# A linear-attention block beside a GEGLU feed-forward: the attention output in four and a half array passes instead of five

## The chip, the cores and the metric

The kernel runs on one core of one Trainium2 chip. The metric is the device time of one execution in microseconds (us); the median of nine runs of the kernel before is 516.6 us, with the lowest at 516.16 and the highest at 517.53. The profile is that of one execution, which took 516.65 us. Its recorded span, from the first to the last instruction that the profile shows, is 514.6 us, so about 2.0 us lie around it.

## The reference

With S = 2048 tokens, D = 576 features, H = 32 heads of Dh = 18 and F = 4608:

```python
xn = layernorm(x)
q, k, v = split_heads(xn @ wqkv)            # (H, S, Dh)
phi = lambda t: where(t > 0, t + 1, exp(t)) + 1e-6
kv  = einsum("hsd,hse->hde", phi(k), v)     # one 18 x 18 matrix for each head
z   = phi(k).sum over s                     # (H, Dh)
num = einsum("hqd,hde->hqe", phi(q), kv)
den = einsum("hqd,hd->hq", phi(q), z) + 1e-6
A   = merge_heads(num / den) @ wo
B   = (gelu(xn @ w_gate) * (xn @ w_up)) @ w_down
out = x + A + B
```

Since the attention is linear, the kernel folds kv and wo into one 576 x 576 matrix M (for each head, kv of the head times the head's 18 rows of wo). With phi(q) divided by its denominators beforehand, the attention output is A = (phi(q)/den) @ M: one more contraction over 576 rows, whose result is added to that of the feed-forward in the same accumulator.

## The kernel before, in words

**Stages.** The first part, up to 68.4 us of the span, does the layer norm, the projections of q and k, the Gram products that give k^T v, and the small matrices kvT (18 x 18 blocks, masked) and zb (z on all partitions). The feed-forward then goes through the tokens in four chunks (`sc`) of 512. In each chunk there are two stages.

- **Gate and up** (`gu_pair`, line 548). 18 blocks `k`, each of two units of 128 hidden columns. A unit makes a gate and an up product in two PSUM banks. The contraction over 576 rows is done by `_Unit` in 64-row tiles of the array: one matmul on rows 0 to 63 (`LO`) and one on rows 64 to 127 (`HI`) run side by side, on different banks (line 309). ScalarE then computes the gelu (line 575), and VectorE multiplies and writes `hT` (line 576).
- **Down** (`down_tile`, line 591). Four tiles `j` of 128 tokens, each in two halves of 288 output columns. A half is 36 full-array passes over `hT` and `w_down` (line 604), then five passes with `pqT` (phi(q)/den, transposed) against `m_sb` (M) (line 609), all into one bank; then VectorE adds x (line 612) and SP sends the tile out (lines 614 and 616).

**The five passes.** The 32 heads are packed 7, 7, 7, 7 and 4 to a chunk (`HCH`), so chunks 0 to 3 fill 126 of the 128 rows, and chunk 4 fills 72. Each chunk is one pass.

**M.** `m_stage` (line 581) makes M, chunk by chunk, within the first half of the first down tile of the first token chunk: before the passes f = 0, 6, 12, 18 and 24 it issues two matmuls of kvT against wo (line 586) into banks that the accumulator does not use, and ScalarE copies each to `m_sb` (line 589).

**Denominators.** For each token tile `n` there are four jobs, kept in the list `den_jobs` (line 546): `den_mul` (line 367), `den_inv` (line 373), `den_scale` (line 379), which are VectorE work and write the padded tile `pn`, and `den_transpose` (line 395), a transposing DMA from `pn` to `pqT` on SP's queue. `gu_pair` takes one job after each unit of the blocks 1 to 16 (line 577). That is 32 jobs in a chunk, so all 64 are done within the first two chunks. The three `pn` buffers are filled with zeros once (line 532), since columns 126 and 127 of the first four chunks, and 72 to 127 of the last, are never written.

**Queues and order.** Nothing is scheduled by a planner in this part: every engine runs its instructions in the order of the code. All loads of weights, the transposes and the stores go through SP's queue. A block's weights are loaded three blocks ahead (`load_gu(blk + NWBUF - 1, i)`, line 565), wo in block 1 of the first chunk (line 569), and w_down in slices in blocks 2 to 13 (line 571). PSUM banks are handed out in a fixed ring of eight (`banks`, line 296), two to each unit and one to each half of a down tile. When a unit's first half is done, `p1` leaves a marker on POOL's queue (line 318), and `p2` waits for it before its row tiles change banks.

Of the kernel before, what the change touches and what calls it, by code (L numbers as in the profile page):

```python
# [9 lines left out]
ALU = mybir.AluOpType  # L10
BF16 = mybir.dt.bfloat16
# [4 lines left out]
P = 128  # L16
HP = 64
S = 2048
D = 576
H = 32  # L20
DH = 18
F = 4608
NS = S // P
NF = F // P
SC = 512
NSC = S // SC
TPC = SC // P
HALF = D // 2
KT = 5
HCH = [7, 7, 7, 7, 4]  # L30
HOFF = [0, 7, 14, 21, 28]
NCH = len(HCH)
CR = 7 * DH
EPS_LN = 1e-5
EPS_ATT = 1e-6
GUB = 2
# [21 lines left out]
def kernel(  # L58
# [11 lines left out]
    nc = tc.nc  # L70
# [5 lines left out]
    out_view = out.flatten_outer_dims().rearrange("(p n) d -> p n d", n=NS)  # L76
# [5 lines left out]
    fwork = ctx.enter_context(tc.tile_pool(name="fwork", bufs=3))  # L82
    psum = ctx.enter_context(tc.tile_pool(name="psum", bufs=1, space=PSUM))

    ps_all = psum.tile([P, 8, 512], F32, name="ps_all")
# [4 lines left out]
    x_sb = persist.tile([P, NS, D], BF16, name="x_sb")  # L90
# [46 lines left out]
    pqT = persist.tile([P, NCH, S], BF16, name="pqT")  # L137
# [5 lines left out]
    hT = h_store[:].rearrange("p (f t) -> p f t", f=NF)  # L143
# [8 lines left out]
    def load_gu(i, part):  # L152

        if i >= NSC * NF // GUB:
            return
        f0 = GUB * (i % (NF // GUB))
        c0, c1 = f0 * P, (f0 + GUB) * P
        if part == 0:
            gu_blocks[i] = (wg_bufs.next(), wu_bufs.next(), wr_bufs.next())
        wg, wu, wr = gu_blocks[i]  # L160
        if part == 0:
            nc.sync.dma_start(wg[:], B_w_gate[0:512, c0:c1].rearrange("(kt p) c -> p kt c", p=P))
            nc.sync.dma_start(wr[0:HP, :], B_w_gate[512:576, c0:c1])
        else:
            nc.sync.dma_start(wu[:], B_w_up[0:512, c0:c1].rearrange("(kt p) c -> p kt c", p=P))
            nc.sync.dma_start(wr[HP:P, :], B_w_up[512:576, c0:c1])
# [13 lines left out]
        out=bm3, in_=bm3, compare_op=ALU.is_ge, fill=0.0,  # L180
# [3 lines left out]
        out=bm3, in_=bm3, compare_op=ALU.is_ge, fill=0.0,  # L184
# [109 lines left out]
    LO, HI = slice(0, HP), slice(HP, P)  # L294
    SYNC = mybir.DependencyInfo(mybir.DependencyClass.Sync, mybir.DependencyReason.DATA)
    banks = _Ring([4, 5, 6, 7, 2, 3, 0, 1])

    class _Unit:
# [5 lines left out]
        def __init__(self, outs, lhs, rhs, relay, first=(4, 0, 1, 2, 3), then=(0, 1, 2, 3)):  # L304
            self.outs, self.lhs, self.rhs, self.relay = outs, lhs, rhs, relay
            self.first, self.then = first, then
# [55 lines left out]
    def heads(ap):  # L362
        return ap.rearrange("p (h e) -> p h e", e=DH)
# [14 lines left out]

    def den_scale(n):
        pn = den_pn[n] = pn_bufs.next()  # L380
        for c0, c1 in ((0, 4), (4, 5)):
            h0, h1 = HOFF[c0], HOFF[c1 - 1] + HCH[c1 - 1]
            nh = HCH[c0]

            def chunked(ap):
                return ap.rearrange("p (c h) e -> p c h e", h=nh)

            nc.vector.scalar_tensor_tensor(  # L388
                out=pn[:].rearrange("p (c t) -> p c t", t=P)[:, c0:c1, :nh * DH].rearrange("p c (h e) -> p c h e", e=DH),
                in0=chunked(heads(pq[:, n, h0 * DH:h1 * DH])), scalar=EPS_ATT,  # L390
                in1=chunked(den_d[n][:, h0:h1].unsqueeze(2).to_broadcast([P, h1 - h0, DH])),
                op0=ALU.add, op1=ALU.mult,
            )

    def den_transpose(n):
        nc.sync.dma_start_transpose(pqT[:, :, n * P:(n + 1) * P], den_pn[n][:])
# [20 lines left out]
    for n in range(NS):  # L417
# [7 lines left out]
        if n < TD:  # L425
            for i, (k0, k1, eng) in enumerate([(0, 3, "ACT"), (3, KT, "ACT" if n else "DVE")]):
                b = TP_BANK[n] - i
# [97 lines left out]
    wd_pool = ctx.enter_context(tc.tile_pool(name="wd", bufs=1))  # L525
    wd_sb = wd_pool.tile([P, NF, D], BF16, name="wd_sb")
    wo2 = wd_pool.tile([P, NCH, D], BF16, name="wo2")
    m_sb = wd_pool.tile([P, NCH, D], BF16, name="m_sb")
    dwork = ctx.enter_context(tc.tile_pool(name="dwork", bufs=1))
    pn_bufs = _Ring([dwork.tile([P, NCH * P], BF16, name=f"pn{i}") for i in range(3)])  # L530
    for pn in pn_bufs.tiles:
        nc.gpsimd.memset(pn[:], 0.0)

    def load_wo():
        nc.sync.dma_start(wo2[:CR, 0:4, :], A_wo[0:4 * CR, :].rearrange("(c p) j -> p c j", p=CR))
        nc.sync.dma_start(wo2[:D - 4 * CR, 4, :], A_wo[4 * CR:D, :])
    wd_loaded = [0]

    def load_wd_slice():
        f0 = wd_loaded[0]  # L540
        if f0 < NF:
            nc.sync.dma_start(wd_sb[:, f0:f0 + WDS, :], wd_view[:, f0:f0 + WDS, :])
            wd_loaded[0] += WDS


    den_jobs = [(job, n) for n in range(NS) for job in (den_mul, den_inv, den_scale, den_transpose)]

    def gu_pair(sc, k):
        cs = slice(sc * SC, (sc + 1) * SC)
        blk = sc * (NF // GUB) + k  # L550
        wg, wu, wr = gu_blocks.pop(blk)
        units = []
        for i in range(GUB):
            b = [banks.next(), banks.next()]
            fcol = slice(i * P, (i + 1) * P)

            def lhs(a, rows, kt, fcol=fcol):
                if kt == 4:
                    return wr[rows, fcol]
                return (wg, wu)[a][rows, kt, fcol]  # L560

            u = _Unit([ps_all[:, b[0], :], ps_all[:, b[1], :]], lhs, lambda a, rows, kt: xnT[rows, kt, cs],
                      nc.sync if blk == 0 else nc.gpsimd)
            if blk > 0:
                load_gu(blk + NWBUF - 1, i)
            u.p1()
            units.append((b, u))
        if sc == 0 and k == 1:
            load_wo()
        elif sc == 0 and k >= 2:  # L570
            load_wd_slice()
        for i, (b, u) in enumerate(units):
            u.p2()
            gl = fwork.tile([P, SC], F32, name="gl")
            nc.scalar.activation(out=gl[:], in_=ps_all[:, b[0], :], func=ACT.Gelu_apprx_tanh)  # L575
            nc.vector.tensor_tensor(out=hT[:, GUB * k + i, :], in0=ps_all[:, b[1], :], in1=gl[:], op=ALU.mult)  # L576
            if den_jobs and 0 < k < NF // GUB - 1:
                job, n = den_jobs.pop(0)
                job(n)

    def m_stage(c, acc_bank):
        rows = DH * HCH[c]
        for hf in range(2):
            b = (acc_bank + 2 + (2 * c + hf) % 6) % 8
            hs = slice(hf * HALF, (hf + 1) * HALF)
            nc.tensor.matmul(  # L586
                ps_all[:rows, b, :HALF], lhsT=kvT[:rows, c, :rows], rhs=wo2[:rows, c, hs], start=True, stop=True,
            )
            nc.scalar.copy(out=m_sb[:rows, c, hs], in_=ps_all[:rows, b, :HALF])

    def down_tile(sc, j, hooks):
        n = sc * TPC + j
        ts_ = slice(n * P, (n + 1) * P)
        res = fwork.tile([P, D], BF16, name="res")
        last = n == NS - 1
        for hf in range(2):
            hs = slice(hf * HALF, (hf + 1) * HALF)
            todo = hooks.pop(0) if hooks else {}
            acc_bank = banks.next()
            acc = ps_all[:, acc_bank, :HALF]  # L600
            for f in range(NF):
                if f in todo:
                    todo[f](acc_bank)
                nc.tensor.matmul(  # L604
                    acc, lhsT=hT[:, f, j * P:(j + 1) * P], rhs=wd_sb[:, f, hs], start=(f == 0), stop=False,
                )
            for c in range(NCH):
                rows = DH * HCH[c]
                nc.tensor.matmul(  # L609
                    acc, lhsT=pqT[:rows, c, ts_], rhs=m_sb[:rows, c, hs], start=False, stop=(c == NCH - 1),  # L610
                )
            nc.vector.tensor_tensor(out=res[:, hs], in0=acc, in1=x_sb[:, n, hs], op=ALU.add)  # L612
            if last:
                nc.sync.dma_start(out_view[:, n, hs], res[:, hs])
        if not last:
            nc.sync.dma_start(out_view[:, n, :], res[:])

    for sc in range(NSC):
        for k in range(NF // GUB):
            gu_pair(sc, k)  # L620
        while wd_loaded[0] < NF:
            load_wd_slice()

        hooks = [{6 * c_: (lambda b, c_=c_: m_stage(c_, b)) for c_ in range(NCH)} if sc == 0 else {}]
        for j in range(TPC):
            down_tile(sc, j, hooks)


# [28 lines left out]
```

## Time and profile before

| what | value |
|---|---|
| median of nine runs | 516.6 us |
| the profiled execution | 516.65 us, span 514.6 us |
| TensorE busy, granted clock | 509.2 us (99%), 1.00 |
| VectorE, ScalarE, POOL busy | 203.0, 136.9, 8.4 us |
| gate and up, each of the four chunks | 70.0 to 70.1 us |
| down, first chunk | 42.0 us |
| down, each of the other chunks | 40.3 to 40.4 us |
| passes of line 604, line 609, line 586 | 1152, 160, 10 |
| DMA share while gate and up of chunks 0, 1, 2, 3 run | 1.01, 0.61, 0.54, 0.46 |

The chain that ended last is TensorE for 97% of the span. The durations of single matmuls in the profile (286 ns for a pass with 288 columns) hold the pipeline's depth; what a pass adds is the distance from one start to the next. DMA share is the mean busy share of the 16 DMA engines.

### The profile page before, as it was taken

The numbers are of one execution on the slowest core, as the hardware profiler recorded it, in microseconds if no ns is written. First come the engines' busy times: TensorE is split into PE (matmuls) and PEld (weight loads), VectorE is DVE, ScalarE is ACT, GpSimd is POOL, SyncE is SP. The second block draws the span as 40 slices with busy tenths as digits, with TensorE's granted clock in tenths as the row PEclk, the third lists the DMA queues.
The fourth block names the chain that finished last, engine by engine and source line by source line (L and its number), as shares of the span: only waits on it lengthen the run. The fifth ranks groups of instructions, "written<-read, shape, count | busy, mean of one in ns | idle before, by whom it ended". The sixth has DMA issues, their size and how long they took to land.

```text
span 514.6 us, 10566 instructions
## 1 busy us (share of the span) xinstructions
PE 509.2 (99%) x4487; PEld 309.3 (60%) x4487; DVE 203.0 (39%) x414; ACT 136.9 (27%) x267; POOL 8.4 (2%) x26
## 2 busy tenths in 40 slices
PE   8999999999999999999999999999999999999997
PEld 7888854444587744444677644444777444445775
DVE  7886447667501046676301133333101234333100
ACT  5887522232410022232100023322000133232000
POOL 3001000000000000000000000000000000000000
PEclk9999999999999999999999999999999999999999
DMA  6543929999900055666400255555100454540000
GB/s 209 144 65 62 247 57 245 272 290 288 206 11 13 13 150 147 183 173 167 128 11 24 59 160 157 145 156 146 33 12 13 129 160 141 160 117 1 13 11 24
DMA packets 118745, 61.02 MB, mean 119 GB/s; under 512 B 25514, under 2 KB 117866, under 8 KB 118698
## 3 DMA queue, kind: packets, MB, share of 16 engines
q1 hardware_dynamic: 118554, 60.20, 44.5%
q8 instruction: 35, 0.57, 0.5%
q10 hardware_dynamic: 144, 0.15, 0.1%
q14 instruction: 12, 0.10, 0.1%
HBM read 52.79 MB, written 2.36 MB: 107 GB/s over the span
## 4 chain that ended last, share of the span: by engine, by line
PE 97%; DMA 1%; SPq 0%; DVE 0%; ACT 0%; issue 0%
PE ps_all L309 54%; PE ps_all L604 27%; PE ps_all L254 7%; PE ps_all L285 4%; PE ps_all L609 4%; DMA wqkv_sb<-in_A_wqkv_dram 1%; PE ps_all L356 0%; PE ps_all L586 0%; SPq L93 0%; DVE hT L576 0%; ACT gl L575 0%; SPq L108 0%; DVE res L612 0%; SPq L107 0%; PE ps_all L346 0%
## 5 line engine op out<-in xcount | busy, mean ns | idle before, releaser
L309 PE MATMUL ps_all<-xnT,wg 64*128 64x512 bf16 x1152 | 271.9, 376 | 0.0
L309 PE MATMUL ps_all<-xnT,wu 64*128 64x512 bf16 x1152 | 271.5, 376 | 0.0
L575 ACT ACTIVATE gl<-ps_all 128x512 f32<-128x512 f32 x144 | 86.0, 597 | 313.6 <-PE ps_all L309 308.8
L576 DVE TENSOR_TENSOR hT<-ps_all,gl 128x512 bf16<-128x512 f32 x144 | 99.3, 690 | 143.6 <-ACT gl L575 143.2
L309 PEld LDWEIGHTS <-wu 64*128 64x128 bf16 x1152 | 108.3, 94 | 68.3
L309 PEld LDWEIGHTS <-wg 64*128 64x128 bf16 x1152 | 108.3, 94 | 67.7
L604 PE MATMUL ps_all<-wd_sb,hT 128*128 128x288 bf16 x1152 | 147.0, 286 | 0.0
L604 PEld LDWEIGHTS <-hT 128*128 128x128 bf16 x1152 | 112.3, 98 | 30.0 <-issue 1.6
L612 DVE TENSOR_TENSOR res<-ps_all,x_sb 128x288 bf16<-128x288 f32 x32 | 14.6, 458 | 144.9 <-PE ps_all L609 144.9
L309 PE MATMUL ps_all<-xnT,wr 64*128 64x512 bf16 x288 | 54.6, 376 | 0.0
L254 PE MATMUL ps_all<-wqkv_sb,xnT 128*128 128x288 bf16 x320 | 42.1, 286 | 0.4 <-ACT xnT L243 0.3
L254 PEld LDWEIGHTS <-xnT 128*128 128x128 bf16 x320 | 30.6, 98 | 7.8 <-ACT xnT L243 0.5
L261 ACT ACTIVATE phi_e<-ps_all,neg 128x288 f32<-128x288 f32 x64 | 30.8, 496 | 9.0 <-PE ps_all L254 6.3
L609 PE MATMUL ps_all<-m_sb,pqT 126*128 126x288 bf16 (+1 forms) x160 | 24.9, 285 | 0.0
L309 PEld LDWEIGHTS <-wr 64*128 64x128 bf16 x288 | 14.0, 94 | 17.4 <-issue 0.7
L285 PE MATMUL ps_all<-hT,xn 128*128 128x288 bf16 (+4 forms) x176 | 22.6, 275 | 0.0
L285 PEld LDWEIGHTS <-xn 128*128 128x128 bf16 (+1 forms) x176 | 17.6, 101 | 3.9
L609 PEld LDWEIGHTS <-pqT 126*128 126x128 bf16 (+1 forms) x160 | 15.5, 97 | 4.1
L266 DVE SCALAR_TENSOR_TENSOR pq<-phi_e,ps_all 128x288 bf16<-128x288 f32 x32 | 14.2, 448 | 7.7 <-ACT phi_e L261 7.2
L266 DVE SCALAR_TENSOR_TENSOR hT<-phi_e,ps_all 128x288 bf16<-128x288 f32 x32 | 14.1, 450 | 2.4 <-ACT phi_e L261 2.3
L203 DVE BATCH_NORM_STATS2 stats<-x_sb 128x6 f32<-128x288 bf16 x32 | 13.6, 440 | 1.9 <-DMA x_sb<-in_A_x_dram 1.9
L388 DVE SCALAR_TENSOR_TENSOR pn<-pq,den_d 128x504 bf16<-128x504 bf16 (+1 forms) x32 | 13.1, 449 | 0.0
(52 smaller groups left out, 96.9 us busy)
## 6 DMA issues: line engine op xcount, KB each, us to landing
wg<-in_B_w_gate_dram SPq DMA_DIRECT2D x72, 256.0 KB, 3.0
wu<-in_B_w_up_dram SPq DMA_DIRECT2D x72, 256.0 KB, 3.6
wd_sb<-in_B_w_down_dram SPq DMA_DIRECT2D x12, 432.0 KB, 4.9
wr<-in_B_w_gate_dram SPq DMA_DIRECT2D x72, 32.0 KB, 2.9
wr<-in_B_w_up_dram SPq DMA_DIRECT2D x72, 32.0 KB, 3.1
out_dram<-res SPq DMA_DIRECT2D x15, 144.0 KB, 1.8
wqkv_sb<-in_A_wqkv_dram SPq DMA_DIRECT2D x3, 576.0 KB, 5.6
x_sb<-in_A_x_dram SPq DMA_DIRECT2D x5, 288.0 KB, 3.2
```

Of the source, the lines that this page charges most:

```text
L203: nc.vector.bn_stats(out=ln_raw[n][:, h, :], in_=x_sb[:, n, h * HALF:(h + 1) * HALF])
L254: nc.tensor.matmul(ps_all[:, KQ_BANK[which] + hf, :HALF], lhsT=xnT[:, kt, n * P:(n + 1) * P], rhs=wqkv_sb[:, kt, c:c + HALF], start=(kt == ...
L261: nc.scalar.activation(out=e[:], in_=ps_all[:, KQ_BANK[which] + hf, :HALF], func=ACT.Exp, bias=neg1[:], scale=1.0,)
L266: nc.vector.scalar_tensor_tensor(out=(pq, pk)[which][:, n, hf * HALF:(hf + 1) * HALF], in0=e_tiles[n, which, hf][:], scalar=1.0, in1=ps_al ...
L285: nc.tensor.matmul(ps_all[:m, b, col:col + w], lhsT=xn[:, n, j0:j0 + m], rhs=pk[:, n, d0:d0 + w], start=(n == 0 and col == 0), stop=(n == ...
L309: return nc.tensor.matmul(self.outs[i], lhsT=self.lhs(i, rows, kt), rhs=self.rhs(i, rows, kt), start=start, stop=stop, skip_group_check=True,)
L388: nc.vector.scalar_tensor_tensor(out=pn[:].rearrange("p (c t) -> p c t", t=P)[:, c0:c1, :nh * DH].rearrange("p c (h e) -> p c h e", e=DH), ...
L575: nc.scalar.activation(out=gl[:], in_=ps_all[:, b[0], :], func=ACT.Gelu_apprx_tanh)
L576: nc.vector.tensor_tensor(out=hT[:, GUB * k + i, :], in0=ps_all[:, b[1], :], in1=gl[:], op=ALU.mult)
L604: nc.tensor.matmul(acc, lhsT=hT[:, f, j * P:(j + 1) * P], rhs=wd_sb[:, f, hs], start=(f == 0), stop=False,)
L609: nc.tensor.matmul(acc, lhsT=pqT[:rows, c, ts_], rhs=m_sb[:rows, c, hs], start=False, stop=(c == NCH - 1),)
L612: nc.vector.tensor_tensor(out=res[:, hs], in0=acc, in1=x_sb[:, n, hs], op=ALU.add)
```

## The change

- Chunk 4 of phi(q) and M keeps 64 rows; its other eight rows go to the free rows 126 and 127 of chunks 0 to 3. `den_scale` does that for phi(q) with one small copy, and with a second one repeats the 64 columns in columns 64 to 127, so that after the transpose they stand on rows 0 to 63 and on rows 64 to 127 of `pqT`. With every column written, the zero fill of `pn` goes.
- For M, chunk 4 is computed early (`m_last_product`, after block 4 of the first chunk) into a tile of its own, `m_last`. Two DMAs after block 7 bring its last eight rows to rows 126 and 127 of chunks 0 to 3 of `m_sb`, and two after block 9 bring the first 64 rows to both halves of chunk 4.
- A half of a down tile then has four full passes with `pqT` instead of five. The 64 rows of chunk 4 are done by `pair()`: one matmul on rows 0 to 63 for the left half, and one on rows 64 to 127 for the right half, on different banks, once for each tile. For tiles 0 and 1 the pairs open the accumulation, directly behind the gate-and-up stage. For tiles 2 and 3 they close it, after the last pass of tile 3 and directly ahead of the next gate-and-up stage; in the last chunk they open it, ahead of tile 2.
- All eight banks of a down stage are taken at its start. Chunks 0 to 3 of M are made ahead of passes 8, 14, 20 and 26, in the banks of tiles 2 and 3.
- `gu_pair` takes one job of `den_jobs` for each block instead of one for each unit: 16 in a chunk, so that a chunk's own four token tiles are prepared in it, and the jobs spread over all four chunks.

```diff
@@ den_scale
+        nc.vector.tensor_copy(
+            out=pn_c[:, 0:4, CR:P], in_=pn_c[:, 4, HP:HP + 8].rearrange("p (i c) -> p c i", c=4),
+        )
+        nc.vector.tensor_copy(out=pn_c[:, 4, HP:P], in_=pn_c[:, 4, 0:HP])
@@
+    m_last = wd_pool.tile([P, D], BF16, name="m_last")
...
-    for pn in pn_bufs.tiles:
-        nc.gpsimd.memset(pn[:], 0.0)
@@ gu_pair
-            if den_jobs and 0 < k < NF // GUB - 1:
+            if den_jobs and i == 1 and 0 < k < NF // GUB - 1:
                 job, n = den_jobs.pop(0)
                 job(n)
@@
-    def m_stage(c, acc_bank):
+    def m_product(c, bank):
...
+    def m_last_product():
+        two = [banks.next(), banks.next()]
+        m_product(4, lambda hf: two[hf])
+
+    def m_last_tails():
+        for i in range(2):
+            nc.sync.dma_start(m_sb[CR + i:CR + i + 1, 0:4, :], m_last[HP + 4 * i:HP + 4 * i + 4, :])
+
+    def m_last_rows():
+        for rows in (LO, HI):
+            nc.sync.dma_start(m_sb[rows, 4, :], m_last[0:HP, :])
+
+    m_last_steps = {4: m_last_product, 7: m_last_tails, 9: m_last_rows}
...
+        def pair(self):
+            for hf, rows in ((0, LO), (1, HI)):
+                nc.tensor.matmul(
+                    self.acc(hf), lhsT=pqT[rows, 4, self.ts], rhs=m_sb[rows, 4, HALVES[hf]],
+                    start=not self.opened, stop=self.opened, skip_group_check=True,
+                )
+            self.opened = True
...
-            for c in range(NCH):
-                rows = DH * HCH[c]
+            for c in range(4):
                 nc.tensor.matmul(
-                    acc, lhsT=pqT[:rows, c, ts_], rhs=m_sb[:rows, c, hs], start=False, stop=(c == NCH - 1),
+                    self.acc(hf), lhsT=pqT[:, c, self.ts], rhs=m_sb[:, c, HALVES[hf]],
+                    start=False, stop=(paired and c == 3), skip_group_check=True,
                 )
...
     for sc in range(NSC):
         for k in range(NF // GUB):
             gu_pair(sc, k)
+            if sc == 0 and k in m_last_steps:
+                m_last_steps[k]()
...
+        tiles = [_DownTile(sc * TPC + j) for j in range(TPC)]
+        tiles[0].pair()
+        tiles[1].pair()
+        spare = tiles[2].banks + tiles[3].banks
+        hooks = {8 + 6 * c: (lambda c=c: m_product(c, lambda hf: spare[(2 * c + hf) % 4])) for c in range(4)} if sc == 0 else {}
+        for j, t in enumerate(tiles):
+            if j == 2 and sc == NSC - 1:
+                tiles[2].pair()
+                tiles[3].pair()
+            closed = t.opened
+            for hf in range(2):
+                t.down(hf, hooks if j == hf == 0 else {})
+                if closed:
+                    t.add(hf)
+        for t in tiles[2:]:
+            if sc < NSC - 1:
+                t.opened = True
+                t.pair()
+                for hf in range(2):
+                    t.add(hf)
```

More of the change, by code (lines that the diff above doesn't have):

```diff
@@ L380, in den_scale @@
         pn = den_pn[n] = pn_bufs.next()
+        pn_c = pn[:].rearrange("p (c t) -> p c t", t=P)
         for c0, c1 in ((0, 4), (4, 5)):
@@ L388, in den_scale @@
             nc.vector.scalar_tensor_tensor(
-                out=pn[:].rearrange("p (c t) -> p c t", t=P)[:, c0:c1, :nh * DH].rearrange("p c (h e) -> p c h e", e=DH),
+                out=pn_c[:, c0:c1, :nh * DH].rearrange("p c (h e) -> p c h e", e=DH),
                 in0=chunked(heads(pq[:, n, h0 * DH:h1 * DH])), scalar=EPS_ATT,
@@ L576, in gu_pair @@
             nc.vector.tensor_tensor(out=hT[:, GUB * k + i, :], in0=ps_all[:, b[1], :], in1=gl[:], op=ALU.mult)
-            if den_jobs and 0 < k < NF // GUB - 1:
+            if den_jobs and i == 1 and 0 < k < NF // GUB - 1:
                 job, n = den_jobs.pop(0)
                 job(n)
-    def m_stage(c, acc_bank):
+    def m_product(c, bank):
         rows = DH * HCH[c]
         for hf in range(2):
-            b = (acc_bank + 2 + (2 * c + hf) % 6) % 8
+            b = bank(hf)
             hs = slice(hf * HALF, (hf + 1) * HALF)
@@ L588, in m_stage @@
             )
[L589 to L600, printed above, removed]
+            nc.scalar.copy(out=m_sb[:rows, c, hs] if c < 4 else m_last[:rows, hs], in_=ps_all[:rows, b, :HALF])
@@ new lines, in m_last_product @@
+    def m_last_product():
[8 more added lines that the diff above has]
+    m_last_steps = {4: m_last_product, 7: m_last_tails, 9: m_last_rows}
+    HALVES = [slice(0, HALF), slice(HALF, D)]
@@ new lines, with __init__, acc, down @@
+    class _DownTile:
+        def __init__(self, n):
+            self.n, self.ts = n, slice(n * P, (n + 1) * P)
+            self.banks = [banks.next(), banks.next()]
+            self.opened = False
+        def acc(self, hf):
+            return ps_all[:, self.banks[hf], :HALF]
+        def pair(self):
[5 more added lines that the diff above has]
+            self.opened = True
+        def down(self, hf, todo):
+            paired = self.opened
+            j = self.n % TPC
@@ L601, in down_tile @@
             for f in range(NF):
                 if f in todo:
-                    todo[f](acc_bank)
+                    todo[f]()
                 nc.tensor.matmul(
-                    acc, lhsT=hT[:, f, j * P:(j + 1) * P], rhs=wd_sb[:, f, hs], start=(f == 0), stop=False,
-                )
-            for c in range(NCH):
-                rows = DH * HCH[c]
+                    self.acc(hf), lhsT=hT[:, f, j * P:(j + 1) * P], rhs=wd_sb[:, f, HALVES[hf]],
+                    start=(f == 0 and not paired), stop=False, skip_group_check=True,
+                )
@@ L609, in down_tile @@
+            for c in range(4):
                 nc.tensor.matmul(
-                    acc, lhsT=pqT[:rows, c, ts_], rhs=m_sb[:rows, c, hs], start=False, stop=(c == NCH - 1),
-                )
[L612 to L616, printed above, removed]
+                    self.acc(hf), lhsT=pqT[:, c, self.ts], rhs=m_sb[:, c, HALVES[hf]],
+                    start=False, stop=(paired and c == 3), skip_group_check=True,
+                )
@@ L618, with add @@
+        def add(self, hf):
+            if hf == 0:
+                self.res = fwork.tile([P, D], BF16, name="res")
+            hs = HALVES[hf]
+            nc.vector.tensor_tensor(out=self.res[:, hs], in0=self.acc(hf), in1=x_sb[:, self.n, hs], op=ALU.add)
+            if self.n == NS - 1:
+                nc.sync.dma_start(out_view[:, self.n, hs], self.res[:, hs])
+            elif hf == 1:
+                nc.sync.dma_start(out_view[:, self.n, :], self.res[:])
     for sc in range(NSC):
@@ L620 @@
             gu_pair(sc, k)
+            if sc == 0 and k in m_last_steps:
+                m_last_steps[k]()
         while wd_loaded[0] < NF:
             load_wd_slice()
-        hooks = [{6 * c_: (lambda b, c_=c_: m_stage(c_, b)) for c_ in range(NCH)} if sc == 0 else {}]
-        for j in range(TPC):
-            down_tile(sc, j, hooks)
+        tiles = [_DownTile(sc * TPC + j) for j in range(TPC)]
[18 more added lines that the diff above has]
+                    t.add(hf)
 _INS = ['A_x', 'A_wqkv', 'A_wo', 'B_x', 'B_w_gate', 'B_w_up', 'B_w_down']
```

## The prediction

> **What bounds the kernel now.** I read the page's busy times first, then the chain that ended last, then the same chain piece by piece in order of time, and last the timeline at the borders of the stages. From the page:
>
> ```profile
> PE 509.2 (99%) x4487; PEld 309.3 (60%) x4487; DVE 203.0 (39%) x414; ACT 136.9 (27%) x267; POOL 8.4 (2%) x26
> PE 97%; DMA 1%; SPq 0%; DVE 0%; ACT 0%; issue 0%
> PE ps_all L309 54%; PE ps_all L604 27%; PE ps_all L254 7%; PE ps_all L285 4%; PE ps_all L609 4%; DMA wqkv_sb<-in_A_wqkv_dram 1%; PE ps_all L356 0%; PE ps_all L586 0%; SPq L93 0%; DVE hT L576 0%; ACT gl L575 0%; SPq L108 0%; DVE res L612 0%; SPq L107 0%; PE ps_all L346 0%
> ```
>
> TensorE is the bound, and it hardly waits: only a pass less, or a wait less, shortens the run. Line 609, the five passes under change, is 4% of the chain. The chain in order of time (start, length, what), at the end of chunk 0's gate and up, and through chunk 1:
>
> ```profile
> 138.47 0.02 issue
> 138.49 0.61 ACT gl L575
> 139.10 0.02 issue
> 139.12 0.70 DVE hT L576
> 139.82 0.04 issue
> 139.87 0.28 PE ps_all L586
> ...
> 180.38 70.04 PE ps_all L309 x648
> 250.42 4.52 PE ps_all L604 x36
> 254.94 0.62 PE ps_all L609 x5
> 255.56 4.41 PE ps_all L604 x36
> ```
>
> Three prices come out of it. A full pass over 288 columns: 4.41/36 = 0.1225 us (line 604), and 0.62/5 = 0.123 (line 609). A side-by-side pair of 64-row matmuls over 512 columns: 70.04 us for 648 chain entries, which are 324 pairs, so 0.216. The change from 64-row tiles to the full array: 4.52 against 4.41, so 0.11 us. The other way is in the timeline: five passes of line 609 start at 289.98, a sixth start would stand at 290.59, and line 309 starts at 290.69, so 0.10. Only in chunk 0 does something else stand in the chain: M's second chunk waits for the last gelu and multiply to free its bank. In the timeline:
>
> ```profile
> 139.41 0.29 PE L586 MATMUL ps_all<-wo,kvT 126*126 126x288 bf16 x1
> 139.87 0.28 PE L586 MATMUL ps_all<-wo,kvT 126*126 126x288 bf16 x1 [0.17 <-DVE hT L576]
> ```
>
> The second matmul starts 0.46 us after the first instead of 0.12: 0.34 us lost.
>
> **What the skill says.** TensorEngine Tiling (Array Packing), Key Properties: changing the tiling mode drains the array. The 0.10 and 0.11 us above agree. TensorE: Matmul & The Clock Gate, Part 3, The mechanism: matmuls on different row tiles overlap, their starts about 4 ns apart, and weight loads overlap where the row group differs. The trace agrees: gate and up matmuls start together (135.70 and 135.70, 135.91 and 135.91), their weight loads at 135.91 and 135.92. Same page, LDWEIGHTS: a load's time goes with columns, not with rows. The trace agrees: 98 ns for 128 rows, 97 ns for 126 and for 72; a 72-row pass is as long as a 126-row one (288 against 285 ns). So the fifth pass, with 72 rows of 128, costs a whole one, and filling rows 126 and 127 costs nothing.
>
> **The change part by part.**
>
> *Passes.* One pass goes from each of 32 halves: 32 x 0.123 = 3.94 us off. Sixteen pairs come. No row shows a 64-row pair with 288 columns. From below it is the column time of one pass, 0.1225, if both run side by side and the loads (94 ns each for 64 rows, side by side) hide as in line 309. From above it is 0.246 if the two run one after the other, and 0.29 with a half-exposed load besides. A gain below 0.12 is excluded, since all 288 columns must stream. I take 0.123, because line 309 does the same on the same rows with different banks: 16 x 0.123 = 1.97 us on.
>
> *Mode changes.* Pairs of tiles 0 and 1 stand directly behind line 309, and those of tiles 2 and 3 directly ahead of it, so the existing changes move and none is added. In the last chunk the pairs ahead of tile 2 add a way in and out: 0.21. `m_last_product` after block 4 adds one too: 0.21. Its two passes are the same two that leave the down stage: 0.
>
> *M.* Moved from f = 0, 6, 12, 18 to 8, 14, 20, 26, into the banks of tiles 2 and 3, that is, of the last block's two units. The last multiplies end at 138.95 and 139.81. The first product now comes at 138.38 + two pairs 0.25 + 8 x 0.1225 = 139.6, the second at 140.6. Both are late enough: 0.34 off. The last copy ends about 0.9 us after the fourth product's start near 142.6, so near 143.6; the first pass that reads M starts at about 144.0. Free, with some 0.4 us to spare.
>
> *`m_last_product`.* It waits for wo and for two banks. Block 4 ends at 68.41 + 5 x 3.89 = 87.9. wo is issued at 74.75 and 75.28. Its landing is not recorded; but each transfer on SP waits for the one eight before it, and the eighth behind wo's second part issues at 83.38, so wo is there by then. The banks are those of block 3's first unit, free. The ring is shifted by one unit from here on: once, block 5's second unit takes the banks of block 4's first one. That unit's gelu starts at 87.12 and its multiply ends at 88.4; the unit starts at about 87.9 + 0.45 + 1.08 = 89.4, so 1.0 us to spare. ScalarE's two copies (0.40 each) follow the gelu that starts at 87.99; the next gelu comes 2.4 us later. Free.
>
> *DMAs.* Four new transfers on SP, about 0.5 us of issue each, in blocks 7 and 9; four transposes with 1.22 us of issue each leave chunk 0, four leave chunk 1, and chunks 2 and 3 get four each. Chunk 0's DMA share is 1.01 before, so it is relieved. In chunks 2 and 3 (0.54, 0.46) the transposes come in at half the rate that chunk 1 took at 0.61 with the same 70.04 us. A late weight load would be the next loss: queued behind a transpose on SP are a block's four loads, but they have three blocks, 11.7 us, and land in 3.0 to 3.6 us. The transposes of tiles 0 to 3 are issued in blocks 4, 8, 12 and 16 and land within 6.7 us at most; the first pairs need the tiles of blocks 4 and 8, the others come ten or more us into the down stage. M's spread rows have from block 9 on, over 30 us.
>
> *VectorE.* Two small copies for each token tile, bounded by the nearest rows, 0.18 (128 x 32) and 0.225 (128 x 72): some 0.4 us inside a block of 3.89 us in which the two multiplies take 1.4 and the longest other job 1.3. VectorE waits 143 us for gelus in all. 0; the zero fill (1.8 us on POOL) also 0, since nothing on the chain waits for it.
>
> *Stage ends.* The adds of tiles 2 and 3 now come together after the last pairs: 4 x 0.46 = 1.84 us, ahead of the next chunk's first multiply, which before came 3.7 us after the stage's end. The stores, and behind them on SP the next loads, issue about 1.6 us later; the loads' 11.7 us cover that. The kernel's end keeps its order: last pass, add, store.
>
> *Sum.* -3.94 + 1.97 + 0.42 - 0.34 = -1.89 us. The profiled span goes from 514.6 to 512.7, its execution from 516.65 to 514.76; that execution is at the median, so the median goes from 516.6 to 514.7 us (-0.37%).
>
> **The rivals.** *Pairs not side by side.* If the two matmuls of a pair, isolated between mode changes, run in turn, 16 x 0.123 come back: 516.7 us. For it: a run of only two pairs has little to hide its loads behind, where line 309 has 324. Against it: both ends of the run join line 309 in the same mode in 7 of 8 cases. No price between 0.123 and 0.24 for a pair turns the gain into a loss.
>
> *wo late, slower.* If wo lands after 87.9, TensorE stands at the product's weight load with everything behind it, and each us late is a us lost. It eats the gain from a landing at 89.8 and gives a loss beyond 0.2% from 90.8; landing at 92, it gives 518.8. For it: the DMA share is 1.01 here, and before the change wo was first read 50 us later. Against it: the 83.38 above, 4.5 us of room, and no added transfer ahead of it.
>
> *No pass leaves the chain* because another engine takes over: against it, VectorE and ScalarE are idle over half of every stage, and the waits for them in the chain sum to the one of 1.4 us.
>
> **How the numbers follow.** A difference of 0.2%, 1.03 us, is about what a measurement of this kernel can tell from none. My forecast has 0.80, with its own range of 514.0 to 515.5: pairs between 0.12 and 0.17, mode changes between 0.05 and 0.15. Pairs dear or in turn: 0.10, around 516.5, most of it within 0.2%. wo late, or another wait of that kind on TensorE: 0.08. More gain than counted: 0.02. The range reaches to 516.2 to take in most of the dear pairs. Faster 0.82, same 0.10, slower 0.08.
>
> **What would show it.** Down stages of about 39.8 us from chunk 1 on and 40.9 in chunk 0, against 40.3 and 42.0; in the last chunk 40.0. 128 passes of the full kind and 32 matmuls of 64 rows, each two starting together. No wait of line 586's kind, no idle TensorE at the product after block 4 beyond 0.2 us. Gate and up unchanged at 70.0, 70.5 in chunk 0 with the product. It is wrong if gate and up grows in any chunk, or if the two starts of a pair lie a pass apart.

## The result, and the profile after

The median went from 516.6 us (31 runs by then) to 514.51 us (10 runs, 514.17 to 515.06): a ratio of 0.9957 with a 95% interval of 0.9949 to 0.9965, or 2.1 us less. The profiled execution has a span of 512.7 us instead of 514.6.

The page of the changed kernel: its busy line, and the chain that ended last by engine and by line.

```profile
PE 507.2 (99%) x4487; PEld 307.5 (60%) x4487; DVE 210.8 (41%) x446; ACT 136.8 (27%) x267; POOL 6.8 (1%) x23
PE 98%; DMA 1%; SPq 0%; DVE 0%; issue 0%
PE ps_all L309 55%; PE ps_all L639 28%; PE ps_all L254 7%; PE ps_all L285 4%; PE ps_all L644 3%; DMA wqkv_sb<-in_A_wqkv_dram 1%; PE ps_all L627 0%; PE ps_all L356 0%; PE ps_all L590 0%; SPq L93 0%; SPq L108 0%; DVE res L653 0%; SPq L107 0%; PE ps_all L346 0%; PE ps_all L239 0%
```

TensorE is the bound as before, with the same number of matmuls, 2.0 us less of them in busy time. The passes of line 604 are now line 639, the four passes line 644 (3%, where the five of line 609 were 4%), the pairs line 627, and M's products line 590. The wait for the last gelu and multiply is gone from chunk 0's down stage; of VectorE only the kernel's last add is left in the chain. VectorE is 7.8 us busier, and no piece of the chain waits for that work.

The same chain in order of time (start, length, what), around the early product, chunk 0's down stage, the border to chunk 1, and the middle of the last chunk:

```profile
68.51 19.53 PE ps_all L309 x180
88.05 0.37 PE ps_all L590 x2
88.41 50.61 PE ps_all L309 x468
139.02 0.24 PE ps_all L627 x4
139.27 1.09 PE ps_all L639 x8
140.35 0.25 PE ps_all L590 x2
...
179.08 0.49 PE ps_all L644 x4
179.57 0.35 PE ps_all L627 x4
179.92 69.93 PE ps_all L309 x648
249.85 0.24 PE ps_all L627 x4
250.09 4.52 PE ps_all L639 x36
...
489.47 0.35 PE ps_all L627 x4
489.82 4.52 PE ps_all L639 x36
```

Four 64-row matmuls behind line 309 add 0.24 us, which is two passes of 0.12 and not four. Ahead of line 309 they show 0.35: the same 0.24 and the way out of the full array, 0.11, which stood before as the first entry's excess of line 309 (70.04 before, 69.93 now).

The timeline of the first pairs shows that their weights come in while line 309 still runs, and that the full array's first weight load starts 0.24 us after the pairs' last one has ended:

```profile
138.64 0.38 PE L309 MATMUL ps_all<-xnT,wu 64*128 64x512 bf16 x1
138.65 0.31 PEld L627 LDWEIGHTS <-pqT 64*128 64x128 bf16 x4
138.65 0.38 PE L309 MATMUL ps_all<-xnT,wg 64*128 64x512 bf16 x1
138.86 0.41 PE L627 MATMUL ps_all<-m_sb,pqT 64*128 64x288 bf16 x4
139.20 0.85 PEld L639 LDWEIGHTS <-hT 128*128 128x128 bf16 x8 [0.24 <-issue]
139.20 1.15 PE L639 MATMUL ps_all<-wd_sb,hT 128*128 128x288 bf16 x8
```

The four matmuls take 0.41 us together, where one alone has 0.285. So the last starts 0.12 us, one pass, after the first: they run two and two.

Where the time went, from the two chains (the stages as the chain borders them):

| stage | before, us | after, us | difference | foretold length |
|---|---|---|---|---|
| gate and up, chunk 0, with the early product | 70.06 | 70.51 | +0.45 | 70.5 |
| down, chunk 0 | 41.91 | 40.90 | -1.01 | 40.9 |
| gate and up, chunks 1 to 3, each | 70.04 | 69.93 | -0.11 | 70.0 |
| down, chunk 1 | 40.34 | 39.90 | -0.44 | about 39.8 |
| down, chunk 2 | 40.33 | 39.90 | -0.43 | about 39.8 |
| down, chunk 3 | 40.35 | 40.03 | -0.32 | 40.0 |

That is -2.08 us in all. The span shows only 1.9, because line 309 happened to start 0.10 us later in this execution (68.51 against 68.41). That start wanders from 68.03 to 68.92 over all the profiled executions of this study, in a part of the kernel whose matmuls no experiment changes. So the experiments are also compared by the stretch from the first matmul of line 309 to the end of the last pass: 443.10 us before (511.51 - 68.41), 441.03 after (509.54 - 68.51). It comes from one execution of each kernel; what is known of its noise is that two pairs of runs below, alike in all that is on the path, agree in it to 0.01 us.

### The profile page after: what moved, and what is told of

Same layout as the page of the kernel before. It is cut to its first block, busy times and chain, and to the rows that moved or that the text cites. A ratio compares the mean times of both kernels' runs of the same rounds, so it can differ in the third digit from the quotient of the medians.

```text
span 512.7 us, 10601 instructions
## 1 busy us (share of the span) xinstructions
PE 507.2 (99%) x4487; PEld 307.5 (60%) x4487; DVE 210.8 (41%) x446; ACT 136.8 (27%) x267; POOL 6.8 (1%) x23
## 4 chain that ended last, share of the span: by engine, by line
PE 98%; DMA 1%; SPq 0%; DVE 0%; issue 0%
PE ps_all L309 55%; PE ps_all L639 28%; PE ps_all L254 7%; PE ps_all L285 4%; PE ps_all L644 3%; DMA wqkv_sb<-in_A_wqkv_dram 1%; PE ps_all L627 0%; PE ps_all L356 0%; PE ps_all L590 0%; SPq L93 0%; SPq L108 0%; DVE res L653 0%; SPq L107 0%; PE ps_all L346 0%; PE ps_all L239 0%
## 5 line engine op out<-in xcount | busy, mean ns | idle before, releaser
L644 PE MATMUL ps_all<-m_sb,pqT 128*128 128x288 bf16 x128 | 20.9, 286 | 0.0
L644 PEld LDWEIGHTS <-pqT 128*128 128x128 bf16 x128 | 12.5, 98 | 3.2
```

The source lines that it names most:

```text
L644: nc.tensor.matmul(self.acc(hf), lhsT=pqT[:, c, self.ts], rhs=m_sb[:, c, HALVES[hf]], start=False, stop=(paired and c == 3), skip_group_ch ...
```

## The experiments

Each stands with its time, the ratio to the kernel before on the same chip, and that stretch. In the diffs, `...` marks code left out.

**Both matmuls of a pair on one row tile.** Theory: the gain rests on the two running side by side. Rival: a pair's time is hidden in the drains, or they take turns already.

```diff
-            for hf, rows in ((0, LO), (1, HI)):
+            for hf, rows in ((0, LO), (1, LO)):
```

> The changed kernel, with both matmuls of a pair on rows 0 to 63, so that they take turns on one row tile; the sums are the same. If the gain rests on the two running side by side, each of 16 pairs costs a second 0.123 us: +1.97 us, down stages 0.49 us longer each, 516.5 us against 514.5, nearly all of the gain gone. If the pairs were already taking turns, or are hidden in the mode changes, nothing changes: 514.5.

516.57 us, ratio 0.9998 (0.9990 to 1.0006); stretch 442.97, so 1.94 us more than the changed kernel. The chain of this experiment at the same border:

```profile
138.96 0.49 PE ps_all L627 x4
139.44 1.09 PE ps_all L639 x8
```

0.49 us for the four instead of 0.24. In the timeline the four take 0.65 us instead of 0.41. The second matmul costs what a pass costs, and nearly the whole gain is gone with it.

**The pairs left out.** The same price from the other side.

```diff
         def pair(self):
-            for hf, rows in ((0, LO), (1, HI)):
-                nc.tensor.matmul(...)
             self.opened = True
...
-            paired = self.opened
+            paired = True
...
-                    start=(f == 0 and not paired), stop=False, skip_group_check=True,
+                    start=(f == 0), stop=False, skip_group_check=True,
```

So the last 64 rows of the contraction are left out, and the first full pass opens each sum.

> The changed kernel without the pairs: the last 64 rows of the attention output's contraction are left out. If a pair costs one pass and the last chunk's isolated one a mode change besides, 16 x 0.123 + 0.21 = 2.2 us less: 512.3. If the pairs lie hidden in the drains at the stage borders, less than 0.5 us changes.

512.15 us, ratio 0.9914 (0.9901 to 0.9927); stretch 438.85, 2.18 us less than the changed kernel. That is 16 pairs at 0.1225 and one way in and out of 0.21 to within a hundredth: the pairs are neither hidden nor dearer than a pass.

**The pairs ahead of their own tile.** Theory: each isolated pair pays a mode change both ways. Rival: the drain hides.

```diff
-        tiles[0].pair()
-        tiles[1].pair()
...
-            if j == 2 and sc == NSC - 1:
-                tiles[2].pair()
-                tiles[3].pair()
+            t.pair()
             closed = t.opened
...
-        for t in tiles[2:]:
-            if sc < NSC - 1:
-                t.opened = True
-                t.pair()
-                for hf in range(2):
-                    t.add(hf)
```

> The changed kernel, with each tile's pair directly ahead of its own passes instead of at the borders of the gate-and-up stages. If a mode change has its price wherever it stands, 12 isolated pairs in place of one double one add 11 ways in and out of 0.21 us: +2.3 us, 516.8. If the drain of a mode change hides behind the queue of passes, or is paid once in a stage, 514.5.

516.85 us, ratio 1.0005 (0.9997 to 1.0013); stretch 443.37, 2.34 us more than the changed kernel, as foretold. The chain at one of the isolated pairs:

```profile
149.60 0.49 PE ps_all L644 x4
150.09 0.23 PE ps_all L627 x2
150.32 4.52 PE ps_all L639 x36
```

0.23 for the pair is 0.12 and a way in of 0.11; 4.52 instead of 4.41 is the way out. An isolated pair costs 0.34 us where the two passes that it replaces cost 0.25. The row tiling gains only where its pairs join a stage that is row-tiled already.

**The early product three times.** Theory: 0.455 us each. Rival: the shifted ring of banks makes units wait.

```diff
-    m_last_steps = {4: m_last_product, 7: ...
+    m_last_steps = {4: m_last_product, 5: m_last_product, 6: m_last_product, 7: ...
```

> The changed kernel, with the product for M's last chunk made three times, after blocks 4, 5 and 6, each in two new banks of the ring and copied again to m_last. The prediction's price is two passes and one way in and out of the full array, 0.245 + 0.21 = 0.455 us each: +0.91 us, 515.4, gate and up of chunk 0 at 71.4. If each shift of the bank ring makes a unit wait for a multiply as well, more than 1.5 us.

515.47 us, ratio 0.9978 (0.9971 to 0.9985); stretch 441.96, 0.93 more than the changed kernel. Gate and up of chunk 0 is 71.45 us. The price holds, and no unit waits for a bank.

**M's products later in the kernel before.** One part of the change alone.

```diff
-        hooks = [{6 * c_: (lambda b, c_=c_: m_stage(c_, b)) ...
+        hooks = [{6 + 6 * c_: (lambda b, c_=c_: m_stage(c_, b)) ...
```

> The kernel before, with M's products ahead of passes 6, 12, 18, 24 and 30 instead of 0, 6, 12, 18 and 24. If the second product's wait for the last multiply is 0.34 us of TensorE's own time, the span shrinks by 0.34 (to about 514.3, run 516.3) and the wait is gone from the chain. If the wait only takes the place of another one (hT's last columns, or the copies of M), the span stays at 514.6.

516.5 us, ratio 0.9996 (0.9988 to 1.0005), which tells nothing at this size, and the span is 514.6 as before. But line 309 started at 68.70 in this execution; the stretch is 442.73, 0.37 us less than before. The chain shows the wait gone:

```profile
68.70 70.04 PE ps_all L309 x648
138.74 0.84 PE ps_all L604 x6
139.58 0.25 PE ps_all L586 x2
139.82 0.74 PE ps_all L604 x6
```

By the chain, the 0.34 us were TensorE's own; the timing alone can't resolve them.

**wo later.** The rival on the other side of the forecast, made to happen.

```diff
-        if sc == 0 and k == 1:
+        if sc == 0 and k == 4:
             load_wo()
-        elif sc == 0 and k >= 2:
+        elif sc == 0 and k >= 1:
             load_wd_slice()
```

> The changed kernel, with wo loaded in block 4 instead of block 1 (a slice of w_down takes its place). The rival that a late wo stops TensorE: issued near 87 and landing 4 to 6 us later, it holds the product behind block 4 for about 4 us, all of it lost: 518 to 520 us, and the chain shows the transfer ahead of the product. If something else covers such a wait, 514.5.

522.73 us, ratio 1.0115 (1.0097 to 1.0133); stretch 449.24, 8.21 us more than the changed kernel. The wait is there, but the loss is more than the wait, and the time lies above the 518 to 520 us expected. The timeline of TensorE (the bracket is the idle time and what ended it), then two windows of 4 us (length; busy time of PE, PEld, DVE, ACT and POOL; granted clock, DMA share, GB/s):

```profile
93.17 0.69 PE L590 MATMUL ps_all<-wo,kvT 72*72 72x288 bf16 x2 [5.19 <-DMA wo<-in_A_wo_dram]
94.20 0.63 PE L309 MATMUL ps_all<-xnT,wg 64*128 64x512 bf16 x1
94.62 0.63 PE L309 MATMUL ps_all<-xnT,wg 64*128 64x512 bf16 x1
```

```profile
92.00:96.00 4.00, 2.83 (x14) 1.04 (x16) 0.00 (x0) 0.69 (x2) 0.00 (x0) 0.56 0.97 231
96.00:100.00 4.00, 4.00 (x26) 1.46 (x24) 0.00 (x0) 0.26 (x1) 0.00 (x0) 0.59 0.13 46
```

After 5.19 us of idle, TensorE ran at about half clock: a pair of line 309 every 0.42 us instead of 0.216, up to 99.3 us of the span. That is the second part of the loss: the rest of gate and up took 53.31 us instead of 50.61, and the product itself 0.3 us more. The Trainium skill says in TensorE: Matmul & The Clock Gate, Part 1, that the clock falls to 4 of 8 pulses after an idle window of about 3.4 us and comes back after a busy one; the 0.42 us agree with the half, the wait of 5.19 us is longer than that window, and the slow stretch, from 93.2 to 99.3 us, is some 6 us long.

**Two denominator jobs for each block, in both kernels.** Theory: the spreading of the jobs is off the path. Rival: it makes the room that M's new transfers need.

```diff
-            if den_jobs and i == 1 and 0 < k < NF // GUB - 1:     # changed kernel
+            if den_jobs and 0 < k < NF // GUB - 1:
```

> The changed kernel, with a denominator job after each unit again, so that all are done in chunks 0 and 1. If spreading the jobs is off the path, 514.5 us and gate and up of chunk 0 at 70.5. If the new transfers of M's rows needed the room on SP and in the DMA that the spreading gave (share 1.01 before in chunk 0), a wait for weights shows in chunk 0 and the time is above 515.5.

```diff
-            if den_jobs and 0 < k < NF // GUB - 1:                # kernel before
+            if den_jobs and i == 1 and 0 < k < NF // GUB - 1:
```

> The kernel before, with one denominator job for each block instead of one for each unit. Off the path: 516.6 us, as before. If the spreading is a part of the gain, 516.0 or less; if transposes in chunks 2 and 3 delay weights, above 517.6.

The kernel before doesn't care: 516.58 us, ratio 0.9998 (0.9989 to 1.0006), stretch 443.10, the same to the hundredth. The changed kernel loses its whole gain: 516.82 us, ratio 1.0000 (0.9992 to 1.0009); stretch 443.21, 2.18 us more. In its chain, gate and up of chunk 0 now runs through VectorE, SP's queue and a transfer (fence one), and TensorE waits for weights (fence two, timeline):

```profile
117.17 0.67 DVE den_d L375
...
118.77 0.62 SPq L163
119.39 0.05 issue
119.44 0.58 SPq L165
120.03 0.04 issue
120.07 3.70 DMA wr<-in_B_w_up_dram
123.77 0.05 issue
123.82 7.09 PE ps_all L309 x63
```

```profile
123.82 0.39 PE L309 MATMUL ps_all<-xnT,wr 64*128 64x512 bf16 x1 [0.26 <-DMA wr<-in_B_w_up_dram]
132.01 0.39 PE L309 MATMUL ps_all<-xnT,wr 64*128 64x512 bf16 x1 [0.26 <-DMA wr<-in_B_w_gate_dram]
132.96 0.39 PE L309 MATMUL ps_all<-xnT,wr 64*128 64x512 bf16 x1 [0.56 <-DVE den_t L369]
132.96 0.09 PEld L309 LDWEIGHTS <-wr 64*128 64x128 bf16 x1 [0.85 <-DMA wr<-in_B_w_up_dram]
```

The profile puts the third wait down to VectorE, but the weight load of the same moment waits for a transfer, as at the other two. From 88 to 141 us the weight loads wait 3.0 us in five places for `wr` (the tile with the last 64 rows of a block's weights), in the kernel before and in the changed one nowhere. Nor is the step from VectorE to SP in fence one shown to be a wait: SP's transpose was under way from 116.87, took 1.22 us as others do, and the `pn` that it moves was finished at 113.2.

How near the edge each kernel is shows in the moment at which SP issues the first load of block 11, that is, of weights for block 14. These are the timelines of before, of the kernel before with one job for each block, of after, and of this experiment:

```profile
114.59 0.77 SPq L162 DMA_DIRECT2D wg<-in_B_w_gate_dram  x1
```

```profile
111.80 0.37 SPq L162 DMA_DIRECT2D wg<-in_B_w_gate_dram  x1
```

```profile
112.31 0.43 SPq L162 DMA_DIRECT2D wg<-in_B_w_gate_dram  x1
```

```profile
118.19 0.53 SPq L162 DMA_DIRECT2D wg<-in_B_w_gate_dram  x1
```

Block 11 itself begins at 111.2, 111.7, 111.8 and 111.5 (the start of line 309, eleven blocks of 3.89 us, and 0.46 where the early product lies ahead). So without M's transfers SP is 3.4 us late with two jobs for each block and 0.1 with one; with them it is 0.5 late with one job, and 6.7 here. The lead is 11.7 us, of which issuing a block's loads (2.4) and landing (3.7) leave, as an estimate, about 5.6.

**Which of the added things overruns the queue.** Four experiments with two jobs for each block: M's transfers in blocks 14 and 15; the transfers on ScalarE's queue; the kernel before with four more transfers; the changed kernel without VectorE's copies (and with the zero fill of `pn` back).

```diff
-    m_last_steps = {4: m_last_product, 7: m_last_tails, 9: m_last_rows}
+    m_last_steps = {4: m_last_product, 14: m_last_tails, 15: m_last_rows}
```

> The changed kernel with a denominator job after each unit, as in the run that lost 2.2 us in chunk 0's gate and up, but with the four transfers of M's rows in blocks 14 and 15, when w_down is all issued. If the loss comes from their place in SP's full queue (some 2.5 us of issue ahead of the weight loads of blocks 7 to 13), it goes: gate and up of chunk 0 at 70.5, 514.5 us. If it comes from VectorE's two extra copies or the shifted bank ring, it stays: 72.7, 516.7 us.

514.64 us, ratio 0.9959 (0.9948 to 0.9971); stretch 441.02, that of the changed kernel. All the loss goes. The copies and the shifted ring are still there, so by themselves they cost nothing.

```diff
             gu_pair(sc, k)
+            if sc == 0 and k == 7:
+                for i in range(2):
+                    nc.sync.dma_start(m_sb[CR + i:CR + i + 1, 0:4, :], wo2[4 * i:4 * i + 4, 4, :])
+            if sc == 0 and k == 9:
+                for rows in (LO, HI):
+                    nc.sync.dma_start(m_sb[rows, 4, :], wo2[0:HP, 4, :])
```

> The kernel before with four more transfers of the same shapes on SP behind blocks 7 and 9 of chunk 0 (rows of wo to rows of m_sb that are not read before they are written again). If the four transfers alone overrun SP's queue when the jobs come two to a block, chunk 0's gate and up grows from 70.1 to about 72.3 and the time to 518.8. If it takes the extra copies of the denominator job as well, 516.6 to 517.2.

518.76 us, ratio 1.0045 (1.0027 to 1.0062); stretch 445.67, 2.57 us more than before. With two jobs for each block, the four transfers are enough, without any copy: two of one partition (1 x 4 x 576) and two of 64 rows, some 0.16 MB in a chunk that moves over 16 MB. The first load of block 11 is issued at 117.94, 7.1 us late.

```diff
-        nc.vector.tensor_copy(out=pn_c[:, 0:4, CR:P], ...)
-        nc.vector.tensor_copy(out=pn_c[:, 4, HP:P], ...)
```

> The changed kernel with a denominator job after each unit, without the two copies in the scale job (pn is filled with zeros once; the moved eight rows and the right half's 64 rows of the contraction are left out). SP's queue as the cause: the loss stays, 516.7 us. VectorE's extra 0.4 us for each token tile as the cause: 514.5 us.

516.65 us, ratio 1.0003 (0.9995 to 1.0011); stretch 442.79, 1.76 us more than the changed kernel instead of 2.18. Most of the loss stays; 0.4 us of the stretch may be the copies', on top of a queue that is late already.

```diff
-            nc.sync.dma_start(m_sb[..., 0:4, :], m_last[...])      # and the two of m_last_rows
+            nc.scalar.dma_start(m_sb[..., 0:4, :], m_last[...])
```

> The changed kernel with a denominator job after each unit, and the four transfers of M's rows issued on ScalarE's queue in blocks 7 and 9 instead of SP's. If SP's time for issuing is what is short, the loss goes: 514.5 us. If it is the DMA engines' time or the completions that later transfers wait for, the loss stays: 516.7.

516.83 us, ratio 1.0006 (0.9998 to 1.0014); stretch 442.98. The loss stays, but this run doesn't settle what it was meant to, since it made a loss of its own. ScalarE's timeline (ACTq is its queue of transfers):

```profile
101.43 4.71 ACTq L601 DMA_DIRECT2D m_sb<-m_last  x2
106.25 2.07 ACT L579 ACTIVATE gl<-ps_all 128x512 f32<-128x512 f32 x4 [5.77 <-DMA m_sb<-m_last]
110.16 3.81 ACTq L605 DMA_DIRECT2D m_sb<-m_last  x2
```

The first two issues take 4.71 us: by the chain, the second is let go by a weight load of SP's queue, issued at 100.08, that lands at 105.52. ScalarE's gelus stand behind the issues, and four of them come late. VectorE's work on `pn` comes late with them, and SP itself then waits from 106.2 to 108.7 us to issue a transpose.

What the four transfers use up, SP's time for issuing, the DMA engines' time or the waits for earlier transfers, stays open. In the changed kernel with two jobs for each block, SP has no pause above 0.22 us from block 4 to block 14, and the four issues take 2.5 us of it. The DMA share tells less: from 88 to 120 us it is 1.05 there, with 264 GB/s, but 1.15, with 279 GB/s, in the run with the transfers in blocks 14 and 15, which loses nothing. That speaks for SP's queue, without showing it.

## Why the prediction was right

The forecast was 514.7 us and a span of 512.7; measured were 514.51 and 512.7. Point by point:

- *Passes and pairs.* One pass at 0.123 less in 32 halves and sixteen pairs at 0.123 more: shown by the run on one row tile (+1.94 against 1.97 foretold) and by the run without pairs (-2.18 against 2.18). The groups of five passes took 0.6175 us on average in the chain and those of four 0.49, so that the saved 4.1 us are a little more than the 3.94 of the sum.
- *Mode changes.* 0.11 each way, at the places named: shown by the pairs set inside the stage (+2.34 against 2.31) and by the product made three times (+0.93 against 0.91).
- *M's wait.* 0.34 us off: shown by the chain of the run on that part alone, with a stretch 0.37 shorter.
- *The early product.* wo was there, the ring's shift cost nothing. The rival with a late wo is real, as the run with the later load shows, and its price was set too low: each us late was to cost one us, and 5.19 us of waiting cost 8.21, since the clock falls as well.
- *DMAs and VectorE at nothing.* Right for the whole change, but here the prediction missed how its parts hang together. It set the four new issues (0.5 us each) against the transposes that leave chunk 0, called the chunk relieved, and did not ask how late SP was: 3.4 us of some 5.6 with two jobs for each block, 0.1 with one. The spreading of the jobs is what pays for M's four transfers. With the jobs at the old rate the changed kernel gives back 2.2 us, and still 1.8 without VectorE's copies. The relief was rightly seen, but that it was large enough was not worked out; so far the zero was luck.
- *Stage ends.* Four adds in a row and later stores: no wait in the chain of chunks 1 to 3; gate and up took 69.93.
- *Readings that were off, without effect on the sum.* VectorE was not idle over half of every stage: in gate and up of chunks 0 and 1 it was busy for 44.3 and 43.4 of 70 us before. That no other engine takes over the chain held all the same. In 7 of 8 cases one end of a run of pairs joins line 309, not both. And the 0.12 us below which a gain is excluded is meant as the price of a pair.

The forecast's chance of 0.80 for the main case stands on prices that the trace before showed, and on one that it did not, that of a pair, which was taken from line 309 and which the run on one row tile bears out. The mechanism that could have spoilt it was named (a late weight load), and put aside by a lead of 11.7 us from which SP's lateness had not been taken off.

## What to carry to other kernels

A contraction that leaves half an array over can be done in row-tiled pairs for different output halves, at one pass for two; but a mode change of 0.11 us each way is nearly a whole pass of 288 columns, so the pairs belong at the border of a stage that is row-tiled anyway. Before a step is costed at nothing because a queue covers it, measure how late that queue already is: the same four small transfers cost nothing where the queue was 0.1 us behind without them, and 1.8 to 2.6 us where it was 3.4. For differences below a us, compare stretches of the trace behind the part that wanders, not spans.

## What was not expected of the hardware

- A TensorE wait of 5.19 us cost 8.2: about 6 us at half clock followed it.
- Four transfers of 0.16 MB in all, two of them of one partition each, put the weight loads 3.3 to 3.7 us further behind and cost the run 1.8 to 2.6 us, in a chunk that moves about 240 GB/s and with SP's queue 3.4 us late before them.
- The first part of the kernel ends up to 0.9 us apart from one profiled execution to another (68.03 to 68.92).
